# Splitting the late weight blocks of an attention and gated-layer kernel during attention, and keeping them in DRAM

## The chip, the cores and the metric

One core of a Trainium2 chip runs the whole program. The metric is device time in microseconds for one execution. The engines are TensorE (PE; PEld is its loading of stationary operands), VectorE (DVE), ScalarE (ACT), GpSimd (POOL) and SyncE (SP), which issues nearly all DMAs. Every engine takes its instructions in the order in which they were written for it, and SP its DMA issues too.

## The reference

```python
# q, k, v: [4, 8, 768, 64]; proj: [64, 6]; w_gate, w_val: [512, 1536]; w_out: [1536, 512]; w_* in float64
q_bits = (einsum('bhsd,dk->bhsk', q, proj) > 0);  k_bits likewise
mask = q_bucket[:, :, :, None] == k_bucket[:, :, None, :]      # bucket: the 6 bits as a number
scores = where(mask, q @ k.T / sqrt(64), -1e9)
attn = softmax(scores);  attn_out = attn @ v
x = attn_out.transpose(0, 2, 1, 3).reshape(3072, 512)
gate = 1 / (1 + exp(-(x @ w_gate)));  val = x @ w_val
return (gate * val) @ w_out
```

## The kernel before

**Attention.** 16 pairs of heads: b from 0 to 3, and hp from 0 to 3 within each b. A pair is done in two groups g = 0, 1 of three 128-row tiles. A tile has scores (sc), a maximum (DVE, into e and st) and an exponential (ACT). A group has transposes of e (tp, copied to ef by ACT or DVE), sums spread by a product (rs, rb), and the product with v (pv). `summed` (DVE) makes xs from pv, and `store` sends xs to the DRAM tensor xd[b], whose second half of columns is g = 1.

**The gated layer** runs over units of 384 tokens: (b, g), eight in all, each of which needs x of all four pairs of b for its g. `load_x` loads x of a unit (xr), ACT makes its high part xh and DVE or GpSimd the low part xl, each in four chunks of 128 features; there is one buffer for xr and one for xh and xl. Every product is taken as three matmuls: high by low, low by high, high by high. The feed-forward width of 1536 is cut into 12 blocks j. `moe_early` does blocks 0 to 3 of all units: zg (gate) and zv (value), `gated` (gf on DVE, gh on ACT, gl on DVE or GpSimd), then zo (three row tiles, 12 matmuls each), which goes to DRAM as part[b]. `moe_late` does blocks 4 to 11 of all units after attention (names with l, and yo), fetches part and adds it. The early part of unit (2,1) is held back until score tile 82 of the 96 is written (HOLD).

**The weights** come as float64 pairs of 32-bit words. `load_w` loads a raw block of 512 KB (rawg, rawv, rawo) and makes its value by integer and float steps: `exponent`, `mantissa`, `whole`, `signed` on DVE, `shifted` on ACT, `scaled` on GpSimd or DVE, and then its high part (`high`, ACT) and low part (`low`, GpSimd or DVE). The 12 early blocks (j < 4, of g, v and o) are made during attention, in buffers that last through the kernel. The 24 late blocks are loaded and made after `switch`, which closes the pools of attention and gives their space to the late weights.

**The order** on every engine is made when the program is built, by a planner (`Plan`). A task has an engine, an assumed duration, a key, and stocks of buffers that it takes and gives. Of the tasks that are ready on an engine, the one with the lowest key is written next. Keys of attention count score tiles; the early units have 1e4, the late ones 2e4, and products that only fill time 1e5. The planner takes 2000 ns and 1 ns for every 200 bytes as the landing time of a DMA, with 600 ns for the issue and at most eight in flight, and orders by these assumptions:

```python
def dma(key, nbytes, emit, **kw):
    return add(key, "sp", 600, emit, tail=2000 + nbytes // 200, **kw)
```

Of the kernel before, what the change touches and what calls it, by code (L numbers as in the profile page):

```python
# [9 lines left out]
F32 = mybir.dt.float32  # L10
F32R = mybir.dt.float32r
BF16 = mybir.dt.bfloat16
I32 = mybir.dt.int32
# [6 lines left out]
P = 128  # L20
# [32 lines left out]
class Plan:  # L53
# [6 lines left out]
    def add(self, key, engine, ns=None, emit=None, after=(), take=(), give=(), tail=0):  # L60
        options = engine if isinstance(engine, list) else [(engine, ns, emit)]
        t = Task((key, len(self.tasks)), options, after, take, give, tail)
        self.tasks.append(t)
        return t
# [80 lines left out]
def lsh_attention_glu_kernel(ctx, tc, q, k, v, proj, w_gate, w_val, w_out, out):  # L145
    nc = tc.nc
    B, H, S, D = q.shape
# [10 lines left out]
    J1 = 4  # L158
# [10 lines left out]
    xd = [dram.tile([HP, P, S], F32, name=f"xd{b}") for b in range(B)]  # L169
    part = [dram.tile([NG, GT, P, DM], F32, name=f"part{b}") for b in range(B)]  # L170


    ps = ctx.enter_context(tc.tile_pool(name="ps", bufs=4, space=PSUM))
    ident = const.tile([P, P], F32, name="ident")
# [52 lines left out]
    def busy():  # L227
        nc.tensor.matmul(idle, zero[:, :P], zero, start=True, stop=True)

    W_KEY, W_STEP = 31.24, 4.87  # L230
    stock = dict(
        one=3, two=2, moe=1, z=2, kr=2, qr=2, vr=2, h=2, e=10, st=3, su=3, rb=2, xs=2,
        ef=14, raw1=1, mid1=1, raw2=2, mid2=2, xr=1, x=1, ob=3,
    )
    plan = Plan(stock)
    add = plan.add
# [6 lines left out]
    def dma(key, nbytes, emit, **kw):  # L243
        return add(key, "sp", 600, emit, tail=2000 + nbytes // 200, **kw)
# [2 lines left out]
    N_EL = KC * P  # L247
    weights = {}
    made = {}

    def load_w(key, n, j, early, after=()):

        z = {}
        raw_name = "raw1" if early else "raw2"
        pools = lambda: (stage1, w1) if early else (later["stage"], later["w"])

        def load():
            z["raw"] = raw = pools()[0].tile([P, 2 * N_EL], I32, name=f"raw{n}{j}", tag="wraw")
            if n == "o":
                nc.sync.dma_start(raw, w_out[j * P : (j + 1) * P, :])
            else:
                w = w_gate if n == "g" else w_val
                nc.sync.dma_start(
                    raw.rearrange("p (c f) -> p c f", c=KC),
                    w[:, 2 * j * P : 2 * (j + 1) * P].rearrange("(c p) f -> p c f", p=P),
                )  # L270
            pairs = raw.rearrange("p (n two) -> p n two", two=2)
            z["low"], z["high"] = pairs[:, :, 0], pairs[:, :, 1]

        def exponent():
            z["ex"] = pools()[0].tile([P, N_EL], I32, name=f"ex{n}{j}", tag="wex")
            nc.vector.tensor_scalar(z["ex"], z["high"], 0x7FF00000, None, op0=ALU.bitwise_and)

        def shifted():
            nc.scalar.activation(z["ex"], z["ex"], AF.Relu, scale=8.0, bias=ebias)

        def mantissa():
            z["mf"] = pools()[0].tile([P, N_EL], I32, name=f"mf{n}{j}", tag="wmf")
            nc.vector.tensor_scalar(
                z["mf"], z["high"], 0x000FFFFF, 0x00100000, op0=ALU.bitwise_and, op1=ALU.bitwise_or
            )

        def whole():
            nc.vector.scalar_tensor_tensor(
                f(z["mf"]), z["low"].bitcast(U32), 2.0**-32, z["mf"], op0=ALU.mult, op1=ALU.add
            )  # L290

        def signed():
            nc.vector.scalar_tensor_tensor(
                z["ex"], z["high"], SIGN, z["ex"], op0=ALU.bitwise_and, op1=ALU.bitwise_or
            )

        def scaled(eng):
            eng.tensor_mul(f(z["ex"]), f(z["mf"]), f(z["ex"]))

        def high():  # L300
            weights[n, j] = tuple(
                pools()[1].tile([P, N_EL], F32R, name=f"w{n}{x}{j}", tag=f"w{n}{x}{j}") for x in "hl"
            )
            nc.scalar.copy(weights[n, j][0], f(z["ex"]))

        def low(eng):
            hi, lo = weights[n, j]
            eng.tensor_sub(lo, f(z["ex"]), f(hi))

        mid = "mid1" if early else "mid2"  # L310
        a = dma(key, 524288, load, after=after, take=[raw_name])
        b1 = add(key, "dve", 340, exponent, after=[a], take=[mid])
        b2 = add(key, "act", 620, shifted, after=[b1])
        c1 = add(key, "dve", 340, mantissa, after=[b1])
        c2 = add(key, "dve", 610, whole, after=[c1])
        d = add(key, "dve", 610, signed, after=[b2, c2], give=[raw_name])
        pick = lambda fn: [("pool", 1230, lambda: fn(nc.gpsimd))] + (
            [] if early else [("dve", 610, lambda: fn(nc.vector))]
        )
        e = add(key, pick(scaled), after=[d])  # L320
        h = add(key, "act", 520, high, after=[e])
        made[n, j] = add(key, pick(low), after=[h], give=[mid])


    sig = mp.tile([P, J1, GN], F32, name="sig")
# [88 lines left out]
    def moe_early(key, b, g, stored, held=()):  # L414

        u = f"{b}_{g}"
        x = load_x(u, b, g, stored)
        prev, zs = held, []
        for j in range(J1):
            z, prev = product(key, u, "g", j, x, prev, False)  # L420
            zs.append(add(
                FIRST, "act", 375, lambda j=j, z=z: nc.scalar.copy(sig[:, j], z["acc"][:, :GN]),
                after=[prev, sig_free[j]], give=z["bank"],
            ))
        s_ = add(FIRST, "act", 3900, lambda: nc.scalar.activation(sig, sig, AF.Sigmoid), after=zs)
        ready = []
        for j in range(J1):
            z, prev = product(key, u, "v", j, x, prev, j == J1 - 1)
            z["gf_free"] = gf_last[0]
            gf_last[0] = gated(u, j, z, prev, s_)  # L430
            ready.append(gf_last[0])
        for t in range(GT):
            z = {}

            def part_(j, t=t, z=z):
                if j == 0:
                    z["acc"] = ps.tile([P, 512], F32, name=f"zo{t}_{u}", tag="one")
                out_product(z["acc"], j, j, t, j == 0, j == J1 - 1)

            def store(eng, t=t, z=z):  # L440
                z["ob"] = mp.tile([P, DM], F32, name=f"ob{t}_{u}", tag="ob", bufs=stock["ob"])
                eng(z["ob"], z["acc"])

            for j in range(J1):
                prev = add(
                    key if j == 0 else OPEN, "pe", 3 * MO, lambda j=j, fn=part_: fn(j), after=[prev, ready[j], made["o", j]],
                    take=["moe", "one"] if j == 0 else [],
                )
            a = add(FIRST, "act", 480, lambda fn=store: fn(nc.scalar.copy), after=[prev] + in_turn["ob"],
                    take=["ob"], give=["moe", "one"])  # L450
            in_turn["ob"] = [a]
            parts[b, g, t] = dma(
                FIRST, 262144, lambda t=t, z=z: nc.sync.dma_start(part[b][g, t], z["ob"]),
                after=[a], give=["ob"],
            )
        for j in range(J1):
            g_free[j] = prev
# [61 lines left out]
    sp = lambda t: t.rearrange("p (j n) -> p j n", j=2)  # L519
    heads = [(b, hp) for b in range(B) for hp in range(HP)]  # L520
    score_tasks = {}
    stored = {b: [] for b in range(B)}
    halves = [slice(0, D), slice(D, P)]


# [87 lines left out]
    def group(i, g, z, needs, v_here):  # L613
# [138 lines left out]
                give=["ef"] * 2 + (["vr"] if c == NC - 1 and g == NG - 1 else []),  # L752
            )
        a = add(n - 4, "dve", 470, summed, after=[prev, spread_], take=["xs"], give=["one", "rb"])
        stored[b].append(dma(n, 196608, store, after=[a], give=["xs"]))

    WARM, FILL = 8, 60
    for m in range(FILL):
# [1 line left out]
    LAG = 4.2  # L760
    for i in range(len(heads)):
        pair(i)
    every = [s_ for b in range(B) for s_ in stored[b]]

    for m, (n, j) in enumerate((n, j) for n in "gvo" for j in range(J1)):
        load_w(W_KEY + W_STEP * m, n, j, True)
    HOLD = len(heads) * NC - 14
    units = [(b, g) for b in range(B) for g in range(NG)]
    for m, (b, g) in enumerate(units):

        moe_early(1e4 + m, b, g, stored[b], score_tasks[HOLD] if (b, g) == (B - 2, NG - 1) else None)

    def switch():
        ph1.close()
        later["stage"] = ctx.enter_context(tc.tile_pool(name="stage2", bufs=2))
        later["w"] = ctx.enter_context(tc.tile_pool(name="w2", bufs=1))
        later["ps"] = ctx.enter_context(tc.tile_pool(name="ps3", bufs=2, space=PSUM))

    later["switch"] = add(0, "sp", 0, switch, after=every + [made[n, j] for n in "gvo" for j in range(J1)],
                          give=["moe"] * 3)  # L780
    for j in range(J1, NJ):
        for n in "gvo":
            load_w(1e3, n, j, False, after=[later["switch"]])
    ends = {}
    for m, (b, g) in enumerate(units):
        moe_late(2e4 + m, b, g, stored[b], ends)
    ends["end"](ends["prev"])

    for _, emit, _, _ in plan.order():
# [31 lines left out]
```

## Time and profile before

| | |
|---|---|
| median of 3 runs | 1177.62 us (1177.05 to 1177.81) |
| profiled execution | 1176.68 us, its span 1174.9 us |
| mean granted clock of TensorE | 0.993 |
| busy, share of the span | PE 97%, DVE 47%, ACT 47%, POOL 19% |
| bytes moved | HBM read 56.63 MB, written 18.87 MB |

The span goes from the first to the last instruction; the execution's time also has what lies around it. In the trace attention ends at about 683 us. The numbers of the sums in the prediction are us from the start of the span. In rows of stretches the numbers after the limits are the length, then busy us and instructions by engine, then granted clock, share of the 16 DMA engines and GB/s.

### The profile page before, as it was taken

How to read it: one execution, taken by the hardware profiler on the slowest of the kernel's cores; microseconds unless marked ns; L12 is line 12 of the kernel's file. 1: busy time of each engine (PE TensorE's matmuls, PEld its weight loads, DVE VectorE, ACT ScalarE, POOL GpSimd, SP SyncE). 2: the span in 40 equal slices, each digit the busy share in tenths (PEclk: the TensorE clock that was granted, in tenths of full speed). 3: DMA queues.
4: the chain of work that ended last, by engine and by line, in shares of the span. 5: the costliest groups of instructions: out<-in, count | busy, mean ns of one | idle time of the engine just before them, and what ended most of it. 6: DMA issues, size and time to landing. Idle time of an engine off the chain costs nothing.

```text
span 1174.9 us, 17438 instructions
## 1 busy us (share of the span) xinstructions
PE 1143.6 (97%) x6999; PEld 876.5 (75%) x7004; DVE 550.0 (47%) x1202; ACT 550.7 (47%) x1094; POOL 218.0 (19%) x190
## 2 busy tenths in 40 slices
PE   9999999999999999999999958899999999999998
PEld 4655657777657777657677647788999999999997
DVE  5777665545465544455545449996020211202021
ACT  4778776546576555576646525533121221212111
POOL 1223100201000201000201026655121221212121
PEclk9999999999999999999999979999999999999999
DMA  7334222211212211211010044452020202202010
GB/s 171 88 105 113 58 65 59 63 39 34 75 55 61 64 39 35 75 55 35 30 46 7 35 139 144 152 161 92 26 81 1 81 4 77 80 2 81 1 54 27
DMA packets 92657, 76.63 MB, mean 65 GB/s; under 512 B 53152, under 2 KB 81824, under 8 KB 92576
## 3 DMA queue, kind: packets, MB, share of 16 engines
q1 hardware_dynamic: 92416, 75.51, 21.5%
q8 instruction: 55, 0.90, 0.3%
q14 instruction: 26, 0.21, 0.1%
q10 hardware_dynamic: 160, 0.00, 0.0%
HBM read 56.63 MB, written 18.87 MB: 64 GB/s over the span
## 4 chain that ended last, share of the span: by engine, by line
PE 85%; DVE 7%; POOL 3%; issue 2%; ACT 2%; DMA 1%; SPq 1%; POOLq 0%; DVEq 0%; ACTq 0%
PE sc L625 12%; PE tp L692 11%; PE pv L703 11%; PE zv_1l L375 5%; PE zg_1l L375 5%; PE yo_1l L408 5%; PE zg L375 5%; PE zv_0l L375 5%; PE zo L408 4%; PE zv L375 4%; PE zg_0l L375 4%; PE yo_0l L408 4%; PE sc L633 2%; PE rs L679 2%; PE hq L561 2%
## 5 line engine op out<-in xcount | busy, mean ns | idle before, releaser
L663 ACT ACTIVATE e<-e,st 128x768 f32<-128x768 f32 x192 | 196.3, 1024 | 44.6 <-DVE st L655 39.3
L643 DVE TENSOR_SCALAR_CACHE_REDUCE e<-sc 128x768 f32<-128x768 f32 x192 | 176.4, 954 | 85.2 <-PE sc L633 80.9
L696 ACT COPY ef<-tp 128x384 f32<-128x384 f32 x278 | 120.4, 486 | 116.7 <-PE tp L692 115.2
L692 PE MATMUL tp<-ident,e 128*128 128x128 f32 x1152 | 154.3, 276 | 0.5 <-ACT ef L696 0.4
L625 PE MATMUL sc<-kt,qt 64*128 64x384 f32 x768 | 149.8, 508 | 0.0
L692 PEld LDWEIGHTS tp<-ident,e 128*128 128x128 f32 x1152 | 127.9, 141 | 28.1 <-issue 19.8
L703 PE MATMUL pv<-ef,vr 128*64 128x384 f32 x768 | 129.6, 487 | 0.0
L625 PEld LDWEIGHTS sc<-kt,qt 64*128 64x128 f32 x768 | 66.1, 186 | 59.6 <-issue 19.6
L703 PEld LDWEIGHTS pv<-ef,vr 128*64 128x64 f32 x768 | 53.7, 137 | 58.3 <-issue 57.7
L391 DVE TENSOR_TENSOR gf_1l<-zv_1l,sig 128x384 f32<-128x384 f32 x32 | 17.8, 558 | 166.5 <-PE zv_1l L375 166.5
L396 POOL TENSOR_TENSOR gl<-gf,gh 128x384 fp32r<-128x384 f32 x29 | 31.0, 1069 | 326.5 <-ACT gh L395 326.5
L391 DVE TENSOR_TENSOR gf_0l<-zv_0l,sig 128x384 f32<-128x384 f32 x32 | 17.8, 555 | 126.1 <-PE zv_0l L375 126.1
L696 DVE COPY ef<-tp 128x384 f32<-128x384 f32 x106 | 56.6, 554 | 42.7 <-PE tp L692 41.9
L507 ACT ACTIVATE sig<-zg_1l 128x384 f32<-128x384 f32 x32 | 15.7, 492 | 96.2 <-PE zg_1l L375 96.2
L396 POOL TENSOR_TENSOR gl<-gf_1l,gh 128x384 fp32r<-128x384 f32 x32 | 33.4, 1045 | 147.6 <-ACT gh L395 147.6
L348 POOL TENSOR_TENSOR xl<-xr,xh 128x384 fp32r<-128x384 f32 x19 | 20.9, 1120 | 194.0 <-ACT xh L345 194.0
L375 PE MATMUL zg<-xh,wgl 128*128 128x384 f32 x128 | 46.8, 366 | 10.2 <-ACT xh L345 10.2
L396 POOL TENSOR_TENSOR gl<-gf_0l,gh 128x384 fp32r<-128x384 f32 x28 | 30.6, 1094 | 108.4 <-ACT gh L395 108.4
L507 ACT ACTIVATE sig<-zg_0l 128x384 f32<-128x384 f32 x32 | 15.6, 489 | 72.2 <-PE zg_0l L375 72.2
L633 PEld LDWEIGHTS <-qb 12*128 12x128 bf16 x384 | 9.6, 90 | 52.3 <-issue 52.3
L375 PE MATMUL zg<-xl,wgh 128*128 128x384 f32 x128 | 45.0, 351 | 3.4 <-DVE xl L348 2.6
L395 ACT CAST gh<-gf_1l 128x384 fp32r<-128x384 f32 x32 | 16.4, 512 | 64.6 <-DVE gf_1l L391 64.6
(148 smaller groups left out, 2508.7 us busy)
## 6 DMA issues: line engine op xcount, KB each, us to landing
vr<-in_v_dram SPq DMA_DIRECT2D x16, 384.0 KB, 3.5
rawg<-in_moe_w_gate_dram SPq DMA_DIRECT2D x12, 512.0 KB, 3.5
xd<-xs SPq DMA_DIRECT2D x32, 192.0 KB, 3.4
rawv<-in_moe_w_val_dram SPq DMA_DIRECT2D x12, 512.0 KB, 3.5
rawo<-in_moe_w_out_dram SPq DMA_DIRECT2D x12, 512.0 KB, 3.5
xr<-xd SPq DMA_DIRECT2D x8, 768.0 KB, 4.8
part<-ob SPq DMA_DIRECT2D x24, 256.0 KB, 2.0
kr<-in_k_dram SPq DMA_DIRECT2D x30, 192.0 KB, 3.7
```

Of the source, the lines that this page charges most:

```text
L375: nc.tensor.matmul(z["acc"][:, :GN], a[:, wc], x[xx][:, c, :], start=(c == 0 and i == 0), stop=(c == KC - 1 and i == 2),)
L391: nc.vector.tensor_mul(z["gf"], z["acc"][:, :GN], sig[:, j])
L396: low = lambda eng: eng.tensor_sub(gl[:, j], z["gf"], f(gh[:, j]))
L408: nc.tensor.matmul(acc, a[:, slot, ts_], w, start=(first and i == 0), stop=(last and i == 2))
L507: lambda slot=slot, z=z: nc.scalar.activation(sig[:, slot], z["acc"][:, :GN], AF.Sigmoid),
L625: nc.tensor.matmul(sc[h][:, j, :GN], z["qt"][rows, c], z["kt"][rows, j * GN : (j + 1) * GN], start=True, stop=False, tile_position=(h * D, 0),
L633: nc.tensor.matmul(sc[h][:, j, :GN], z["qb"][rows, c], z["kb"][rows, :], start=False, stop=True, tile_position=(at_, 0),)
L643: nc.vector.tensor_scalar(sp(e), gz["sc", t][h][:, :, :GN], -SCALE, None, op0=ALU.mult, op1=ALU.min, accum_out=gz["st", t][:, 0, h : h + 1],)
L663: nc.scalar.activation(e, e, AF.Exp, bias=st[:, 2, h : h + 1], scale=st[:, 1, h : h + 1], accum_out=gz["su"][:, h, t : t + 1],)
L692: nc.tensor.transpose(tp[:, t * P : (t + 1) * P], gz["e", t, h][:, c * P : (c + 1) * P], ident)
L696: copy(gz["ef", c, h], gz["tp", c, h][:, :GN])
L703: nc.tensor.matmul(gz["pv"][rows, :GN], z["v"][:, h, c], gz["ef", c, h], start=(c == 0), stop=(c == NC - 1), tile_position=(0, h * D),)
```

## The change

All 24 late blocks are now loaded and split during attention, on the same buffers as the early ones (one raw, one of intermediate values), after the 12 early blocks. `scaled` and `low` are always on GpSimd. High and low part of a block stand in one tile; a late block's tile (wk, one buffer) is stored in a DRAM tensor `kept` of its own (`keep`, 512 KB in rows of 4 KB). After `switch` each late block is fetched from there (`fetch`, 512 KB) into its place, and nothing more is done to it. The keys of the blocks start at 12.0 and go up by 2.2. A unit (b, g), early or late, waits for the four stores of its own g in place of all eight of b. `switch` waits for all stores of attention and all 24 `keep`s.

```diff
+    kept = {(n, j): dram.tile([P, 2, DM], F32, name=f"k{n}{j}") for n in "gvo" for j in range(J1, NJ)}
...
-    W_KEY, W_STEP = 31.24, 4.87
+    W_KEY, W_STEP = 12.0, 2.2
...
-        ef=14, raw1=1, mid1=1, raw2=2, mid2=2, xr=1, x=1, ob=3,
+        ef=14, raw1=1, mid1=1, wk=1, xr=1, x=1, ob=3,
...
         def high():
-            weights[n, j] = tuple(
-                pools()[1].tile([P, N_EL], F32R, name=f"w{n}{x}{j}", tag=f"w{n}{x}{j}") for x in "hl"
-            )
-            nc.scalar.copy(weights[n, j][0], f(z["ex"]))
+            if early:
+                z["w"] = w1.tile([P, 2, N_EL], F32R, name=f"w{n}{j}", tag=f"w{n}{j}")
+                weights[n, j] = z["w"][:, 0], z["w"][:, 1]
+            else:
+                z["w"] = stage1.tile([P, 2, N_EL], F32R, name=f"w{n}{j}", tag="wk", bufs=stock["wk"])
+            nc.scalar.copy(z["w"][:, 0], f(z["ex"]))
...
+        def keep():
+            nc.sync.dma_start(kept[n, j], f(z["w"]))
+
+        def fetch():
+            w = later["w"].tile([P, 2, N_EL], F32R, name=f"w{n}{j}", tag=f"w{n}{j}")
+            weights[n, j] = w[:, 0], w[:, 1]
+            nc.sync.dma_start(f(w), kept[n, j])
...
+        e = add(key, "pool", 1230, lambda: scaled(nc.gpsimd), after=[d])
+        h = add(key, "act", 520, high, after=[e], take=[] if early else ["wk"])
+        made[n, j] = add(key, "pool", 1230, lambda: low(nc.gpsimd), after=[h], give=["mid1"])
+        if not early:
+            a = dma(key, 524288, keep, after=[made[n, j]], give=["wk"])
+            fetches.append(((n, j), a, fetch))
...
-        stored[b].append(dma(n, 196608, store, after=[a], give=["xs"]))
+        stored[b, g].append(dma(n, 196608, store, after=[a], give=["xs"]))
...
-        moe_early(1e4 + m, b, g, stored[b], score_tasks[HOLD] if (b, g) == (B - 2, NG - 1) else None)
+        moe_early(1e4 + m, b, g, stored[b, g], score_tasks[HOLD] if (b, g) == (B - 2, NG - 1) else None)
...
-    later["switch"] = add(0, "sp", 0, switch, after=every + [made[n, j] for n in "gvo" for j in range(J1)],
+    later["switch"] = add(0, "sp", 0, switch, after=every + [a for _, a, _ in fetches],
                           give=["moe"] * 3)
-    for j in range(J1, NJ):
-        for n in "gvo":
-            load_w(1e3, n, j, False, after=[later["switch"]])
+    for w, a, fetch in fetches:
+        made[w] = dma(1e3, 524288, fetch, after=[a, later["switch"]])
```

SP at the end of attention, before. xd3 with xs3_3_0 and xs3_3_1 are the stores of the last two groups, xr3_0 and xr3_1 the loads of x of units (3,0) and (3,1), and raw the raw weight blocks with their j:

```order
L713 DMA xd3_65<-xs3_3_0_7080 128x384
L713 DMA xd3_65<-xs3_3_1_7173 128x384
L338 DMA xr3_0_7176<-xd3_65 128x4x384
L267 DMA rawg4_7190<-in_moe_w_gate_dram 128x4x256
L267 DMA rawv4_7192<-in_moe_w_val_dram 128x4x256
L264 DMA rawo4_7218<-in_moe_w_out_dram 128x1024
L338 DMA xr3_1_7231<-xd3_65 128x4x384
```

The same place now, where kg4 is the kept tensor of block 4 of the gate and wg4 its place in SBUF:

```order
L722 DMA xd3_65<-xs3_3_0_7426 128x384
L347 DMA xr3_0_7504<-xd3_65 128x4x384
L722 DMA xd3_65<-xs3_3_1_7523 128x384
L318 DMA wg4_7552<-kg4_70 128x1024
L347 DMA xr3_1_7557<-xd3_65 128x4x384
L318 DMA wv4_7562<-kv4_78 128x1024
L318 DMA wo4_7569<-ko4_86 128x1024
```

The load of x of unit (3,0) has moved ahead of the last store, and no raw load stands at this place.

SP further on, around the load of x of the first late unit (xr0_0l), before:

```order
L264 DMA rawo5_7322<-in_moe_w_out_dram 128x1024
L267 DMA rawg6_7378<-in_moe_w_gate_dram 128x4x256
L267 DMA rawv6_7422<-in_moe_w_val_dram 128x4x256
L338 DMA xr0_0l_7430<-xd0_62 128x4x384
L264 DMA rawo6_7469<-in_moe_w_out_dram 128x1024
L453 DMA part3_69<-ob0_3_0_7490 128x512
```

And now:

```order
L318 DMA wg11_7702<-kg11_77 128x1024
L318 DMA wv11_7708<-kv11_85 128x1024
L318 DMA wo11_7717<-ko11_93 128x1024
L347 DMA xr0_0l_7743<-xd0_62 128x4x384
L462 DMA part3_69<-ob0_3_0_7772 128x512
L462 DMA part3_69<-ob1_3_0_7793 128x512
```

Before, eight of the 24 raw loads were ahead of this x; now all 24 fetches are, and the stores of part come behind it.

ACT around the conversion of that x (xh0_0l), before:

```order
L304 CAST wvh7_7656<-exv7_7597 128x512
L395 CAST gh_136<-gf1_3_1_7662 128x384
L345 CAST xh0_0l_7671<-xr0_0l_7430 128x384 x4
L395 CAST gh_136<-gf2_3_1_7680 128x384
L279 ACTIVATE exg8_7705<-exg8_7705,ebias_92 128x512
L395 CAST gh_136<-gf3_3_1_7707 128x384
```

And now:

```order
L404 CAST gh_160<-gf1_3_1_7887 128x384
L354 CAST xh0_0l_7901<-xr0_0l_7743 128x384 x3
L404 CAST gh_160<-gf2_3_1_7909 128x384
L354 CAST xh0_0l_7901<-xr0_0l_7743 128x384
L404 CAST gh_160<-gf3_3_1_7933 128x384
L516 ACTIVATE sig_159<-zg4_0_0l_7913 128x384
L451 COPY ob0_3_1_7957<-zo0_3_1_7897 128x512
```

The steps of the weights are gone from here; the conversion stands ahead of the last two gh of unit (3,1), as it did.

More of the change, by code (lines that the diff above doesn't have):

```diff
@@ L249, in lsh_attention_glu_kernel, with load_w @@
     made = {}
-    def load_w(key, n, j, early, after=()):
+    fetches = []
+    def load_w(key, n, j, early):
         z = {}
-        raw_name = "raw1" if early else "raw2"
-        pools = lambda: (stage1, w1) if early else (later["stage"], later["w"])
         def load():
-            z["raw"] = raw = pools()[0].tile([P, 2 * N_EL], I32, name=f"raw{n}{j}", tag="wraw")
+            z["raw"] = raw = stage1.tile([P, 2 * N_EL], I32, name=f"raw{n}{j}", tag="wraw")
             if n == "o":
@@ L274, in exponent @@
         def exponent():
-            z["ex"] = pools()[0].tile([P, N_EL], I32, name=f"ex{n}{j}", tag="wex")
+            z["ex"] = stage1.tile([P, N_EL], I32, name=f"ex{n}{j}", tag="wex")
             nc.vector.tensor_scalar(z["ex"], z["high"], 0x7FF00000, None, op0=ALU.bitwise_and)
@@ L281, in mantissa @@
         def mantissa():
-            z["mf"] = pools()[0].tile([P, N_EL], I32, name=f"mf{n}{j}", tag="wmf")
+            z["mf"] = stage1.tile([P, N_EL], I32, name=f"mf{n}{j}", tag="wmf")
             nc.vector.tensor_scalar(
@@ L300, in high @@
         def high():
-            weights[n, j] = tuple(
-                pools()[1].tile([P, N_EL], F32R, name=f"w{n}{x}{j}", tag=f"w{n}{x}{j}") for x in "hl"
-            )
-            nc.scalar.copy(weights[n, j][0], f(z["ex"]))
-        def low(eng):
[L307 to L312, printed above, removed]
+            if early:
[4 more added lines that the diff above has]
+            nc.scalar.copy(z["w"][:, 0], f(z["ex"]))
+        def low(eng):
+            eng.tensor_sub(z["w"][:, 1], f(z["ex"]), f(z["w"][:, 0]))
+        def keep():
[4 more added lines that the diff above has]
+            nc.sync.dma_start(f(w), kept[n, j])
+        a = dma(key, 524288, load, take=["raw1"])
+        b1 = add(key, "dve", 340, exponent, after=[a], take=["mid1"])
         b2 = add(key, "act", 620, shifted, after=[b1])
@@ L315, in load_w @@
         c2 = add(key, "dve", 610, whole, after=[c1])
[L316 to L322, printed above, removed]
+        d = add(key, "dve", 610, signed, after=[b2, c2], give=["raw1"])
+        e = add(key, "pool", 1230, lambda: scaled(nc.gpsimd), after=[d])
[4 more added lines that the diff above has]
+            fetches.append(((n, j), a, fetch))
     sig = mp.tile([P, J1, GN], F32, name="sig")
@@ L521, in lsh_attention_glu_kernel @@
     score_tasks = {}
-    stored = {b: [] for b in range(B)}
+    stored = {(b, g): [] for b in range(B) for g in range(NG)}
     halves = [slice(0, D), slice(D, P)]
@@ L762, in lsh_attention_glu_kernel @@
         pair(i)
-    every = [s_ for b in range(B) for s_ in stored[b]]
-    for m, (n, j) in enumerate((n, j) for n in "gvo" for j in range(J1)):
-        load_w(W_KEY + W_STEP * m, n, j, True)
+    every = [a for s_ in stored.values() for a in s_]
+    order = [(n, j) for n in "gvo" for j in range(J1)] + [(n, j) for j in range(J1, NJ) for n in "gvo"]
+    for m, (n, j) in enumerate(order):
+        load_w(W_KEY + W_STEP * m, n, j, j < J1)
     HOLD = len(heads) * NC - 14
@@ L769, in lsh_attention_glu_kernel @@
     for m, (b, g) in enumerate(units):
-        moe_early(1e4 + m, b, g, stored[b], score_tasks[HOLD] if (b, g) == (B - 2, NG - 1) else None)
+        moe_early(1e4 + m, b, g, stored[b, g], score_tasks[HOLD] if (b, g) == (B - 2, NG - 1) else None)
     def switch():
         ph1.close()
-        later["stage"] = ctx.enter_context(tc.tile_pool(name="stage2", bufs=2))
         later["w"] = ctx.enter_context(tc.tile_pool(name="w2", bufs=1))
         later["ps"] = ctx.enter_context(tc.tile_pool(name="ps3", bufs=2, space=PSUM))
-    later["switch"] = add(0, "sp", 0, switch, after=every + [made[n, j] for n in "gvo" for j in range(J1)],
+    later["switch"] = add(0, "sp", 0, switch, after=every + [a for _, a, _ in fetches],
                           give=["moe"] * 3)
-    for j in range(J1, NJ):
-        for n in "gvo":
-            load_w(1e3, n, j, False, after=[later["switch"]])
+    for w, a, fetch in fetches:
+        made[w] = dma(1e3, 524288, fetch, after=[a, later["switch"]])
     ends = {}
     for m, (b, g) in enumerate(units):
-        moe_late(2e4 + m, b, g, stored[b], ends)
+        moe_late(2e4 + m, b, g, stored[b, g], ends)
     ends["end"](ends["prev"])
```

## The prediction

> **What bounds the kernel now.** I read the page first, then the waits of TensorE, then its busy time stage by stage.
>
> ```profile
> span 1174.9 us, 17438 instructions
> PE 1143.6 (97%) x6999; PEld 876.5 (75%) x7004; DVE 550.0 (47%) x1202; ACT 550.7 (47%) x1094; POOL 218.0 (19%) x190
> PE 85%; DVE 7%; POOL 3%; issue 2%; ACT 2%; DMA 1%; SPq 1%; POOLq 0%; DVEq 0%; ACTq 0%
> ```
>
> TensorE is the bound: 97% busy, 85% of the chain that ended last. The number of matmuls does not change, so only the time in which TensorE stands or runs slowly can be won. The stretches below give busy time by engine (PE, PEld, DVE, ACT, POOL), granted clock, DMA share and GB/s. The third to fifth rows run from the end of attention on.
>
> ```profile
> 57.30:140.00 82.70, 82.15 (x607) 48.48 (x608) 60.88 (x158) 66.58 (x141) 20.37 (x16) 1.00 0.32 91
> 160.00:400.00 240.00, 240.00 (x1632) 167.65 (x1631) 125.64 (x315) 146.50 (x292) 20.32 (x21) 1.00 0.21 58
> 682.99:707.18 24.19, 11.87 (x49) 10.64 (x50) 13.88 (x19) 7.47 (x14) 9.10 (x6) 0.72 0.52 171
> 707.20:815.00 107.80, 97.03 (x483) 86.08 (x482) 99.41 (x123) 51.43 (x92) 65.13 (x46) 0.98 0.41 132
> 815.00:1170.00 355.00, 353.73 (x1843) 327.34 (x1843) 60.05 (x90) 66.21 (x136) 72.32 (x68) 1.00 0.14 45
> ```
>
> Attention keeps TensorE full (0.55 us lost in the first row, none in the second). After the late weights are done it is full again (1.27 us lost in 355). The loss lies between 683 and 815, where DVE is 92% busy (99.41 of 107.8) with the late blocks. The waits of TensorE over the whole run (total, times, longest) name who is late there:
>
> ```profile
> PE zg L375 <- ACT xh L345: 10.2, 1, 10.2
> PE zo L408 <- DVE gl L396: 3.9, 3, 1.8
> PE zg L375 <- DVE xl L348: 2.6, 2, 1.4
> PE zv_0l L375 <- DVE gf_0l L391: 1.9, 1, 1.9
> PE zo L408 <- POOL gl L396: 1.5, 2, 1.4
> PE yo_0l L408 <- DVE gl L396: 1.2, 2, 0.8
> ```
>
> The first is the load of x for unit (3,0). It stands in SP's queue behind the store of the last group, and runs beside two raw weight blocks. The others are DVE and GpSimd busy with the split.
>
> **What goes.** The rows of TensorE at the seam, then clock and DMA there:
>
> ```profile
> 678.90 4.04 PE L703 MATMUL pv<-ef,vr 128*64 128x384 f32 x24
> 693.18 0.69 PE L375 MATMUL zg<-xh,wgl 128*128 128x384 f32 x1 [10.24 <-ACT xh L345]
> 707.18 0.33 PE L375 MATMUL zv<-xh,wvl 128*128 128x384 f32 x1
> 715.50 0.39 PE L408 MATMUL zo<-woh,gl 128*128 128x512 f32 x1
> 715.73 0.40 PE L408 MATMUL zo<-wol,gh 128*128 128x512 f32 x1
> ...
> 688.00:690.00 2.00, 0.00 (x0) 0.00 (x0) 0.00 (x0) 0.00 (x0) 0.00 (x0) 0.52 0.96 310
> 702.00:704.00 2.00, 2.00 (x13) 2.00 (x12) 0.57 (x1) 0.79 (x2) 1.72 (x1) 1.00 1.07 386
> 718.00:720.00 2.00, 1.34 (x4) 0.92 (x5) 2.00 (x2) 0.00 (x0) 2.00 (x2) 0.70 0.00 0
> 720.00:722.00 2.00, 2.00 (x8) 1.81 (x7) 2.00 (x4) 0.52 (x1) 0.36 (x2) 0.50 0.05 7
> 686.00:690.00 4.00, 0.00 (x0) 0.00 (x0) 0.00 (x0) 0.00 (x0) 0.00 (x0) 0.76 0.97 325
> ```
>
> Between 707.18 and 715.50 lie 48 products: 8.32 us, 0.173 each. A zo product takes 0.23 (715.50 to 715.73). So:
> - Standing from 682.99 (the last pv's end without its drain) to 693.18: 10.2 us.
> - The 48 zg products of unit (3,0) take 14.0 us (693.18 to 707.18) where 8.3 would do, in holes and at a clock near 0.5: 5.7 us.
> - Idle from 707.2 to 815 (107.80 less 97.03): 10.8 us.
> - The clock at 718 to 722: half of 2.0 busy us, and 0.3 of 1.34: 1.4 us.
>
> Together 28.1 us, as far as their causes go: no raw load beside x, no split on DVE and GpSimd after 683.
>
> **What comes, term by term.**
>
> (a) x for (3,0) now waits for the store of its own half alone. These rows time it (timeline; chain of waits, start and us; DMA issues with median us to landing; groups with busy us and mean ns):
>
> ```profile
> 674.25 0.56 DVE L710 TENSOR_TENSOR xs<-pv,rb 128x384 f32<-128x384 f32 x1 [2.47 <-PE pv L703]
> 674.84 0.32 SPq L713 DMA_DIRECT2D xd<-xs  x1
> 683.65 1.90 DMA xd<-xs
> 686.13 6.54 DMA rawv<-in_moe_w_val_dram
> xd<-xs SPq DMA_DIRECT2D x32, 192.0 KB, 3.4
> rawo<-in_moe_w_out_dram SPq DMA_DIRECT2D x12, 512.0 KB, 3.5
> xr<-xd SPq DMA_DIRECT2D x8, 768.0 KB, 4.8
> L345 ACT CAST xh<-xr 128x384 fp32r<-128x384 f32 x32 | 14.8, 510 | 4.6 <-POOL gl L396 4.6
> L348 POOL TENSOR_TENSOR xl<-xr,xh 128x384 fp32r<-128x384 f32 x19 | 20.9, 1120 | 194.0 <-ACT xh L345 194.0
> ```
>
> The store is issued at 675.2, lands at 677.1 to 678.6 (1.9 to 3.4), x lands 4.8 later, xh takes 0.5 and xl 1.1. The second product can then start at 683.5 to 685.0, TensorE is there at 683.0: 0.5 to 2.5 us with the later chunks, taken 1.3.
>
> (b) The units start a group of heads earlier, so zo of unit (2,1), which fills gaps in the last pair before, is done by then; the last group and a half of attention have nothing beside them. The nearest row is the bare first stretch, with 0.55 us lost in 82.7: -0.5 (the first bare stretch is shorter now) to 2, taken 0.5.
>
> (c) 24 blocks are split during attention. Four blocks of one kind, exponent tile, then mantissa tile (DVE, ACT and POOL; DVE and POOL):
>
> ```profile
> 0.00:145.00 145.00, 4.43 (x8) 5.29 (x8) 10.17 (x8) 1.00 0.40 106
> 0.00:145.00 145.00, 4.46 (x8) 5.09 (x4) 1.00 0.40 106
> ```
>
> So a block costs DVE (4.43+4.46)/4 = 2.2 us, ACT 1.3, POOL 2.5 (the second row's POOL time is in the first already); 24 cost 53, 32 and 61. They are covered: from 160 to 400 DVE is 52% busy, ACT 61%, POOL 8%. If the cover fails, TensorE waits for st, ef and e. In 57.30 to 140, where 8 blocks (16 POOL instructions) were split beside bare attention with DVE at 74% and ACT at 81%, 0.55 us were lost: 24 at that rate are 1.7. SP also gets 24 stores; each waits for POOL with loads of q, k, v, x and the stores of attention behind it, and 12.6 MB more are written beside a DMA share of 0.2 to 0.3. Two buffers of q, k and v cover a late load; a late x would stop TensorE. 0 to 5 (three times the nearest row), taken 1.0.
>
> (d) Units (3,0) and (3,1) still follow each other with the chain gf, gh, gl, and x of the second can be converted only when the first lets go. Nearest rows: 1.27 us in 355 without split work, and 5.4 for zo with it: 0.4 to 3, taken 1.5.
>
> (e) **The unhidden one.** In SP's order the 24 fetches, of 524 KB each, stand ahead of the load of x for the first late unit. Behind the issue at 685.6 (the last store lands: 683.65 + 1.90) go 24 fetches, x of (3,1) and x of (0,0): 14.16 MB. At 325 GB/s, the 4 us row above, that is 43.6 us; with 1.9 fixed (3.5 for 512 KB less 1.6 at that rate) x lands at 731.1, and the second product can start 1.6 later, at 732.7. From 684.3, with (a), TensorE has 192 zg and zv products of the two units and 42 of zo ahead of it: 192 x 0.1735 + 42 x 0.23 = 43.0 us, and with (d) it is there at 728.8. So 2.9 us and some for chunks: 3.5. The ends: at 386 GB/s (the row at 702) x lands in time: 0. At 212 GB/s, the lowest rate of a full queue, below, x lands at 754.3: 27. I take 325, the same queue at the same place with rows of 1 KB and more. While ACT waits for this x, gh of (3,1) and sig stand behind it, and on SP the part stores; TensorE would wait for the x at that point anyway.
>
> (f) The clock fell about 5 us after the stop at 683, but also at 718 after two waits of 1.3 and 0.7. Taken 0.7, ends 0 and 3.
>
> Sum: 1.3 + 0.5 + 1.0 + 1.5 + 3.5 + 0.7 = 8.5, so 28.1 - 8.5 = 19.6 us are won. The profiled execution took 1176.68; 1176.68 - 19.6 = 1157.1. The median of the runs is 0.94 above it: 1158.0.
>
> The Trainium skill, DMA: Bandwidth & Descriptors, section Bandwidth, puts the limit of transfers between HBM and SBUF at about 358 GB/s for a core. By it the 14.16 MB take an estimated 39.6 us, 4 less, term (e) is 0 and the sum 1154.5; the trace's 325 at a share of 0.97 leans to that side of my value, its 386 goes past it.
>
> **Rivals.**
> 1. The fetches are hidden, and TensorE reaches late unit (0,0) after its x: (e) and (f) are 0, (c) and (d) at their low ends: 1152. The row of 386 GB/s speaks for it, that of 325 against.
> 2. The split in attention is not covered: an in-order engine or SP's queue, waiting for POOL, holds back e, ef or an x load. Half a microsecond for each of the 24 blocks: 12 in place of 1.0, 1169. The bare stretch speaks against it.
> 3. The seam stays: x of (3,0) is late all the same, since its store and load queue behind others. Half the old stop, 5, and half the loss at the clock, 3, in place of 1.3: 1165. Against it: no raw block is in SP's queue there any more.
> 4. The other side: the train of fetches is slow. Slower than before begins where (e) reaches 3.5 + 19.6 = 23, that is 14.16 MB in 63.2 us, 224 GB/s. This row is the longest full queue in the trace:
>
> ```profile
> 0.00:20.00 20.00, 17.65 (x85) 8.36 (x86) 10.31 (x41) 5.91 (x10) 1.17 (x7) 1.00 0.95 212
> ```
>
> At 212 GB/s (e) is 27 and (f) 3: 1158.0 + 23.5 + 2.3 = 1184. These were loads of q and k in rows of 256 bytes, those of the fetch have 4 KB, so I give it little. [...]
>
> **Chances and range.** My forecast, 1154 to 1163: 0.54. Rival 1: 0.19. Rival 2: 0.12. Rival 3: 0.08. Rival 4: 0.07. A measurement of this kernel can tell about 0.2%, 2.4 us, from no change. Rivals 1 and 3, the forecast and most of 2 are faster: 0.92; 0.02 within; 0.06 slower. The range of 1151 to 1168 leaves out rival 4 and half of rival 2.
>
> **What would show it.** TensorE's wait for xh at the seam falls from 10.2 to under 2 us, and no stretch there has a clock near 0.5 for more than 4 us. DVE is under 30% busy from 685 to 815. TensorE stays full from 60 to 680; if its idle time there is over 5 us, (c) is wrong. From 686 the DMA share is near 1 for about 43 us; xr_0l lands near 731, and the largest single wait of TensorE is zg_0l on xh_0l or xl_0l at about 729, of some 3 us. If that wait is over 10 us the fetch rate was wrong, if there is none, rival 1 holds. I would be most wrong where the fetch train runs far below 325 GB/s.

## The result and the profile after

| | before | after |
|---|---|---|
| median | 1177.34 us (1176.76 to 1177.81, 4 runs) | 1150.50 us (1150.28 to 1150.98, 4 runs) |
| ratio | | 0.9773, 95% interval 0.9756 to 0.9790 |
| profiled execution | 1176.68 us, span 1174.9 | 1150.42 us, span 1148.6 |
| mean granted clock of TensorE | 0.993 | 1.0 |
| HBM read, written | 56.63, 18.87 MB | 69.21, 31.46 MB |

The change wins 26.8 us. The prediction said 1158.0 (1151 to 1168): 7.5 us too slow, and half a microsecond outside its range. Of the 7.5, 0.9 lie outside the span: the prediction put the median of the runs 0.94 above the profiled execution, as it was before, and it is 0.08 above it. The page after, first the span, the busy times and the chain that ended last:

```profile
span 1148.6 us, 17525 instructions
PE 1138.4 (99%) x6999; PEld 873.8 (76%) x7004; DVE 501.1 (44%) x1182; ACT 548.6 (48%) x1093; POOL 231.5 (20%) x211
PE 93%; POOL 2%; ACT 2%; DMA 1%; DVE 1%; issue 1%; POOLq 0%; SPq 0%; DVEq 0%; ACTq 0%
```

TensorE has the same 6999 matmuls and now fills 99% of the span. All its waits after the start of the program (total, times, longest) fit into four rows:

```profile
PE zg L384 <- DVE xl L357: 1.0, 2, 0.6
PE tp L701 <- ACT ef L705: 0.8, 2, 0.4
PE zg_0l L384 <- DVE xl_0l L357: 0.4, 1, 0.4
PE yo_1l L417 <- POOL gl L405: 0.3, 1, 0.3
```

Neither xh at the seam (10.2 us before) nor xh_0l, for which the prediction had the largest wait, is among them. The stretches, columns as before:

```profile
57.30:140.00 82.70, 82.22 (x606) 48.50 (x608) 61.11 (x160) 67.03 (x142) 20.37 (x16) 1.00 0.33 97
160.00:400.00 240.00, 239.49 (x1608) 166.25 (x1606) 168.43 (x399) 167.02 (x326) 77.77 (x65) 1.00 0.46 150
57.30:680.00 622.70, 621.47 (x4256) 419.65 (x4256) 382.40 (x952) 416.23 (x830) 124.77 (x106) 1.00 0.30 95
683.00:815.00 132.00, 130.23 (x682) 119.23 (x679) 22.59 (x34) 34.83 (x66) 27.15 (x26) 1.00 0.40 151
690.00:720.00 30.00, 29.50 (x157) 27.35 (x156) 4.74 (x7) 11.06 (x19) 5.21 (x5) 1.00 1.03 408
```

Attention carries all 36 blocks (DVE 168.43 us busy in 160 to 400, 125.64 before) and TensorE loses 1.2 us in 622.7. From 683 to 815 DVE is 17% busy; before, it was 92% busy in the stretch from 707.2 to 815. In 690 to 720 the fetches move 408 GB/s. SP's issues of the first fetch and of the load of x for late unit (0,0), and that load's time to landing:

```profile
687.52 0.32 SPq L318 DMA_DIRECT2D wg<-kg  x1
714.78 0.37 SPq L347 DMA_DIRECT2D xr_0l<-xd  x1
xr_0l<-xd SPq DMA_DIRECT2D x1, 768.0 KB, 11.1
```

It lands at 714.78 + 11.1 = 725.9. ACT converts it only at 728.90, when the last zv of unit (3,1) lets go of the one buffer for xh:

```profile
728.90 1.34 ACT L354 CAST xh_0l<-xr_0l 128x384 fp32r<-128x384 f32 x3 [2.86 <-PE zv L384]
```

So this load has 3.0 us to spare. TensorE's rows at the same points as those shown of before, at that late unit, and at the start of the second late unit (0,1):

```profile
680.80 4.04 PE L712 MATMUL pv<-ef,vr 128*64 128x384 f32 x24
684.77 0.44 PE L384 MATMUL zg<-xh,wg 128*128 128x384 f32 x1
686.56 0.44 PE L384 MATMUL zg<-xl,wg 128*128 128x384 f32 x1 [0.60 <-DVE xl L357]
...
694.31 0.33 PE L384 MATMUL zv<-xh,wv 128*128 128x384 f32 x1
...
728.65 0.39 PE L417 MATMUL zo<-wo,gl 128*128 128x512 f32 x1
728.88 0.63 PE L417 MATMUL zo<-wo,gh 128*128 128x512 f32 x2
730.04 0.33 PE L384 MATMUL zg_0l<-xh_0l,wg 128*128 128x384 f32 x1
...
786.04 0.33 PE L384 MATMUL zg_1l<-xh_1l,wg 128*128 128x384 f32 x1
```

The start of the second late unit before:

```profile
812.41 0.33 PE L375 MATMUL zg_1l<-xh_1l,wgl 128*128 128x384 f32 x1
```

The gap from the last pv to the first zg is 3.97 us, the length of the pv itself; it was 14.28. By the starts of TensorE's matmuls (zv of (3,0) at 707.18 before and 694.31 after, zg_1l of (0,1) at 812.41 and 786.04), the gain stands in these places:

| place | before | after | won | by the prediction |
|---|---|---|---|---|
| last pv starts | 678.90 | 680.80 | -1.9 | -1.5 (b, c) |
| last pv to zv of (3,0): the seam | 28.28 | 13.51 | 14.8 | 14.6 (10.2 + 5.7 - a) |
| zv of (3,0) to zg_1l of (0,1) | 105.23 | 91.73 | 13.5 | 6.5 (12.2 - d, e, f) |
| the rest of the span | 362.5 | 362.6 | -0.1 | 0 |
| sum | | | 26.3 | 19.6 |

The first two places came out nearly as predicted. What is missing stands in the third.

### The profile page after: what moved, and what is told of

The parts are those of the page before. It is cut to its first block, busy times and chain, and to the rows that moved or that the text cites. A ratio compares the mean times of both kernels' runs of the same rounds, so it can differ in the third digit from the quotient of the medians.

```text
span 1148.6 us, 17525 instructions
## 1 busy us (share of the span) xinstructions
PE 1138.4 (99%) x6999; PEld 873.8 (76%) x7004; DVE 501.1 (44%) x1182; ACT 548.6 (48%) x1093; POOL 231.5 (20%) x211
## 3 DMA queue, kind: packets, MB, share of 16 engines
HBM read 69.21 MB, written 31.46 MB: 88 GB/s over the span
## 4 chain that ended last, share of the span: by engine, by line
PE 93%; POOL 2%; ACT 2%; DMA 1%; DVE 1%; issue 1%; POOLq 0%; SPq 0%; DVEq 0%; ACTq 0%
PE sc L634 12%; PE tp L701 11%; PE pv L712 11%; PE zv_0l L384 6%; PE zv_1l L384 6%; PE zo L417 6%; PE zg_0l L384 5%; PE zg_1l L384 5%; PE zv L384 5%; PE yo_0l L417 5%; PE zg L384 5%; PE yo_1l L417 5%; PE rs L688 2%; PE sc L642 2%; PE hq L570 2%; PE idle L230 1%
## 5 line engine op out<-in xcount | busy, mean ns | idle before, releaser
L672 ACT ACTIVATE e<-e,st 128x768 f32<-128x768 f32 x192 | 196.3, 1024 | 49.7 <-DVE st L664 48.6
L384 PE MATMUL zg<-xh,wg 128*128 128x384 f32 x256 | 72.2, 344 | 0.0
L384 PE MATMUL zv<-xh,wv 128*128 128x384 f32 x256 | 71.5, 344 | 0.0
L384 PE MATMUL zg_1l<-xh_1l,wg 128*128 128x384 f32 x256 | 70.9, 337 | 0.0
L384 PE MATMUL zg_0l<-xh_0l,wg 128*128 128x384 f32 x256 | 70.8, 337 | 0.0
L384 PE MATMUL zv_0l<-xh_0l,wv 128*128 128x384 f32 x256 | 70.3, 334 | 0.0
L384 PE MATMUL zv_1l<-xh_1l,wv 128*128 128x384 f32 x256 | 70.2, 334 | 0.0
L405 POOL TENSOR_TENSOR gl<-gf_0l,gh 128x384 fp32r<-128x384 f32 x32 | 33.7, 1055 | 145.1 <-ACT gh L404 145.1
L516 ACT ACTIVATE sig<-zg_1l 128x384 f32<-128x384 f32 x32 | 15.7, 492 | 96.3 <-PE zg_1l L384 96.3
```

The costliest lines, as they stand in the source:

```text
L384: nc.tensor.matmul(z["acc"][:, :GN], a[:, wc], x[xx][:, c, :], start=(c == 0 and i == 0), stop=(c == KC - 1 and i == 2),)
L405: low = lambda eng: eng.tensor_sub(gl[:, j], z["gf"], f(gh[:, j]))
L672: nc.scalar.activation(e, e, AF.Exp, bias=st[:, 2, h : h + 1], scale=st[:, 1, h : h + 1], accum_out=gz["su"][:, h, t : t + 1],)
```

## Experiments

**One part alone: waiting for the own half.** The kernel before, with the list of stores kept by half:

```diff
-        stored[b].append(dma(n, 196608, store, after=[a], give=["xs"]))
+        stored[b, g].append(dma(n, 196608, store, after=[a], give=["xs"]))
...
-        moe_late(2e4 + m, b, g, stored[b], ends)
+        moe_late(2e4 + m, b, g, stored[b, g], ends)
```

The early units' line is changed in the same way.

> The kernel before with one part of the change: units wait for the four stores of their own half; the late blocks are still loaded and split after attention. Theory A (two losses, one behind the other, DVE sets the end of the first late unit): x of unit (3,0) comes in time and TensorE's wait for xh at the seam falls from 10.2 us to under 2, but the split of the 24 blocks still ends at about 810 us with DVE over 90% busy, so that unit (0,0) of the late part ends where it did: the time is 1172 to 1177 us, a gain of at most 5. Rival B (the losses add up): the 13 us of the seam are won whole, 1163 to 1166 us.

Measured: 1179.72 us (1177.05 to 1180.61), 1.0018 [1.0009, 1.0028] of the kernel before: 2 us slower, where even Theory A had a small gain. The wait for xh at the seam is gone (first zg at 684.65), but the waits of TensorE have others at their head, and the stretch after 707 is still DVE's:

```profile
PE zg_0l L375 <- POOL wgl L308: 7.5, 2, 4.8
PE yo_0l L408 <- POOL gl L396: 2.3, 1, 2.3
707.00:815.00 108.00, 93.22 (x422) 82.27 (x420) 98.09 (x122) 47.40 (x84) 60.11 (x45) 0.89 0.41 134
```

DVE has as much to do there as before, 98 us in 108 (99.41 in 107.8). TensorE, earlier at the late units, stands for wgl, and the clock in the stretch falls to 0.89 (0.98 before). The 13 us won at the seam are all given back: zv of (3,0) starts at 693.88 in place of 707.18, but zg_1l of (0,1) at 813.14 in place of 812.41. Where the last 2 us went is not shown.

**The other part alone.** The changed kernel, whose units wait for both halves:

```diff
-        moe_early(1e4 + m, b, g, stored[b, g], score_tasks[HOLD] if (b, g) == (B - 2, NG - 1) else None)
+        moe_early(1e4 + m, b, g, stored[b, 0] + stored[b, 1], score_tasks[HOLD] if (b, g) == (B - 2, NG - 1) else None)
...
-        moe_late(2e4 + m, b, g, stored[b, g], ends)
+        moe_late(2e4 + m, b, g, stored[b, 0] + stored[b, 1], ends)
```

> The changed kernel with units waiting for all eight stores again: only the split during attention, the keeping and the fetching are left of the change. Theory A: the seam's stop comes back in part, x of (3,0) is loaded behind the last store and lands at about 691 us; TensorE waits about 7 us for xh, its clock falls for 2 to 4 us, and the bare last group is filled again (-1): 1158 to 1161 us. Rival B (the losses add up): 1150.5 + 13 = 1163 to 1165 us. Rival C (the train of fetches lies beside this x load and holds it up like the raw loads did): 1163 us or more, with the wait for xh over 9 us.

Measured: 1156.88 us (1155.80 to 1157.42), ratio 0.9826 [0.9812, 0.9841]: 20.9 us by itself, a little more than expected. The stop at the seam stays, with its low clock:

```profile
PE zg L384 <- ACT xh L354: 6.5, 1, 6.5
686.00:688.00 2.00, 0.00 (x0) 0.00 (x0) 0.00 (x0) 0.00 (x0) 0.00 (x0) 1.00 0.87 255
688.00:690.00 2.00, 0.00 (x0) 0.00 (x0) 0.00 (x0) 0.54 (x2) 0.00 (x0) 0.63 1.03 375
690.00:692.00 2.00, 1.58 (x4) 1.19 (x5) 1.58 (x2) 1.21 (x3) 1.95 (x2) 0.50 1.01 389
692.00:694.00 2.00, 2.00 (x8) 2.00 (x7) 0.74 (x1) 0.00 (x0) 0.32 (x1) 0.50 1.02 414
694.00:696.00 2.00, 2.00 (x10) 2.00 (x9) 0.00 (x0) 0.48 (x1) 0.00 (x0) 0.67 1.03 420
```

So the parts don't add up: -2.0 and 20.9 us apart, 26.8 together. The own half is worth 6 us only where no split follows the seam.

**The train made longer.** Behind each fetch, SP also issues a copy of the same block into another DRAM tensor:

```diff
             nc.sync.dma_start(f(w), kept[n, j])
+            nc.sync.dma_start(extra[n, j], kept[n, j])
```

> The changed kernel with a copy of 512 KB from DRAM to DRAM behind each of the 24 fetches, 12.6 MB more ahead of the load of x of the first late unit; the copies are read by nothing. Theory A (at 408 GB/s that load is only 3 to 5 us ahead of its use): 26.7 MB take 65 us, TensorE waits 25 to 30 us for xh_0l or xl_0l, 1175 to 1182 us. Rival B (the train has much room): TensorE waits under 5 us, 1150 to 1155 us.

Measured: 1178.24 us (1176.90 to 1178.98), ratio 1.0004 [0.9995, 1.0013]: the whole gain is gone.

```profile
PE zg_0l L386 <- ACT xh_0l L356: 25.6, 1, 25.6
720.00:750.00 30.00, 11.37 (x64) 10.76 (x62) 1.11 (x2) 3.08 (x5) 2.02 (x2) 0.74 1.01 423
```

The wait that the prediction spoke of is the one that appears. In the changed kernel the train is hidden, but only by the 3.0 us between the landing of x at 725.9 and its conversion at 728.9.

**No split at all.** The late blocks are neither loaded nor split; what is kept and fetched in their place is the early block of the same matrix with number j mod 4, so the values of the late products are others:

```diff
-            nc.sync.dma_start(kept[n, j], f(z["w"]))
+            nc.sync.dma_start(kept[n, j], f(tiles[n, j % J1]))
...
+        if not early:
+            a = dma(key, 524288, keep, after=[made[n, j % J1]])
+            fetches.append(((n, j), a, fetch))
+            return
```

> The changed kernel without the loading and splitting of the 24 late blocks: what is kept and fetched for block j is the split early block j modulo 4, so the late part multiplies by other weights. All 24 stores and fetches remain. Theory A (term (c): the split beside attention costs the 1 to 2 us by which attention ends later than before): attention ends at 683 to 683.5 us in place of 685.0, 1148.5 to 1149 us. Rival B (term (b): the bare last group costs them): it ends at 685 as now, 1150.2 to 1150.8 us.

Measured: 1149.63 us (1149.14 to 1149.97), ratio 0.9766 [0.9749, 0.9782], between the two theories. The last pv starts at 680.29, in place of 680.80: 24 blocks loaded and split beside attention cost 0.5 us there and 0.9 in the total. With the own half alone the last pv started at 680.68, with the split alone (units waiting for both halves) at 679.46. So most of the 1.9 us by which attention ends later than before (678.90) belongs to the new order of the units, not to the split.

**The rows of the kept tensors.** The same bytes are laid out so that a store or a fetch moves rows of 1 KB, 512 or 256 bytes in place of 4 KB (here 1 KB):

```diff
-    kept = {(n, j): dram.tile([P, 2, DM], F32, name=f"k{n}{j}") for n in "gvo" for j in range(J1, NJ)}
+    kept = {(n, j): dram.tile([4, P, DM // 2], F32, name=f"k{n}{j}") for n in "gvo" for j in range(J1, NJ)}
...
-            nc.sync.dma_start(f(w), kept[n, j])
+            nc.sync.dma_start(
+                f(w).rearrange("p h (c e) -> p (h c) e", c=2), kept[n, j].rearrange("c p e -> p c e")
+            )
```

> The changed kernel with the kept blocks laid out so that keep and fetch move rows of 1 KB in place of 4 KB; bytes and number of DMAs are the same. Theory A (the 325 GB/s at the seam of the kernel before came from rows of 1 and 1.5 KB, the 408 of the fetches from rows of 4 KB): the train runs at 320 to 350 GB/s and takes 40 to 44 us, x of the first late unit lands at 730 to 734 us, TensorE waits 2 to 5 us for xh_0l, 1153 to 1156 us. Rival B (the rate hangs on how many DMAs are queued, not on the rows): over 400 GB/s, no such wait, 1150 to 1151 us.

> The same with rows of 512 bytes. Theory A: a rate between 212 and 350 GB/s, near 280: 14.16 MB take 50.6 us, x of the first late unit lands near 740 and TensorE waits about 10 us: 1158 to 1166 us. Theory B: as with 1 KB rows, 350 GB/s and a wait near 2 us: 1153 to 1156 us.

> The late blocks are kept in DRAM so that a store or a fetch moves rows of 256 bytes; nothing else differs from the changed kernel. Theory A: the row's size sets the rate of the train (256-byte rows of q and k moved at 212 GB/s at the program's start, 1 KB rows of the train at 350, 4 KB rows at 408). Then 14.16 MB from about 687.5 take 66.8 us, x of the first late unit lands near 756 and TensorE, free at 730, waits some 26 us for it, with 1 to 3 more at a lower clock: 1176 to 1181 us, so that the change would be worth nothing. Theory B: the 212 belonged to the program's start (few queues filled, rows spread over all heads) and the train runs near 350 GB/s as with 1 KB rows: 1153 to 1156 us.

Of the three kernels in this order, the waits and the same 30 us of the train, and with 1 KB rows also ACT's conversion of the late x, which now starts when that x lands:

```profile
PE zg_0l L388 <- ACT xh_0l L358: 2.2, 1, 2.2
732.39 0.93 ACT L358 CAST xh_0l<-xr_0l 128x384 fp32r<-128x384 f32 x2 [5.77 <-DMA xr_0l<-xd]
690.00:720.00 30.00, 29.50 (x157) 27.33 (x156) 4.74 (x7) 11.07 (x19) 5.22 (x5) 1.00 1.09 350
```

```profile
PE zg_0l L388 <- ACT xh_0l L358: 9.7, 1, 9.7
690.00:720.00 30.00, 29.49 (x157) 27.33 (x156) 4.75 (x7) 11.08 (x19) 5.23 (x5) 1.00 1.11 294
```

```profile
PE zg_0l L388 <- ACT xh_0l L358: 24.0, 1, 24.0
690.00:720.00 30.00, 29.51 (x157) 27.35 (x156) 4.75 (x7) 11.09 (x19) 5.23 (x5) 1.00 1.23 223
```

| row | GB/s in 690 to 720 | wait for xh_0l | median us | ratio |
|---|---|---|---|---|
| 4 KB | 408 | none | 1150.50 | 0.9773 [0.9756, 0.9790] |
| 1 KB | 350 | 2.2 | 1154.05 (1153.22 to 1154.60) | 0.9800 [0.9783, 0.9816] |
| 512 B | 294 | 9.7 | 1161.96 (1161.36 to 1162.36) | 0.9865 [0.9850, 0.9880] |
| 256 B | 223 | 24.0 | 1175.49 (1174.09 to 1177.36) | 0.9984 [0.9975, 0.9994] |

The row's size, of stores and fetches together, moves the kernel from the full gain to nearly none. Attention has little part in it: the last pv starts at 681.42, 681.57 and 681.16, 0.4 to 0.8 us later than with 4 KB. At 512 and 1024 bytes the time lies where Theory A put it; at 256 it lies 0.5 us below that, with the train at 223 GB/s where 212 had been taken.

**How long unit (2,1) is held back.** Its early part, whose zo can fill gaps at the end of attention, is released at another score tile, four later (-10 in place of -14) and in a second kernel ten later (-4):

```diff
-    HOLD = len(heads) * NC - 14
+    HOLD = len(heads) * NC - 10
```

> The changed kernel with the early part of unit (2,1) held back until score tile 86 in place of 82, so that its zv and zo stand between the products of the last pair. Theory A (most of the 1.9 us by which attention ends later come from the last group and a half having nothing beside it): attention ends 1 to 1.5 us earlier, 1149 to 1149.6 us. Rival B (a stretch is bare either way, a pair earlier now, and costs the same): 1150.3 to 1151 us.

> The changed kernel with that unit held until score tile 92: its zo (36 products, 8.2 us) stands between the last pv and zg of unit (3,0), and a pair's worth of attention before is bare. Theory A: the conversion of x of (3,0) is covered by that zo, so the 1.2 us of holes in zg go, and the bare stretch costs what it does now: 1149 to 1149.6 us. Rival B: the longer bare stretch costs more than that, 1151 us or over.

Measured: 1150.12 us (1149.94 to 1150.35) and 1150.58 (1150.27 to 1150.65), ratios 0.9769 [0.9754, 0.9783] and 0.9772 [0.9757, 0.9787]. Theory A's earlier end of attention is not there: with -10 the last pv starts at 681.06 (680.80 in the changed kernel). With -4 it starts at 673.14, and the zo products held back fill the time up to the first zg at 685.41 (684.77 in the changed kernel): they change places, and the sum stays. Theory A's gain is not measured, and neither is the loss that Rival B had for -4. The place of that work is worth 0.4 us at most.

## Why the prediction was off

**The bound.** Right: a gain could only come from TensorE's standing and slow running between 683 and 815, and it came from there and nowhere else.

**(a), the seam.** Right: 14.8 us won there, 14.6 predicted. xh was in time; the xl of a later chunk is waited for by 0.6 at 686.56.

**(b) and (c), attention.** 1.9 us in place of 1.5. The parts were the other way round: the split, given 1.0, costs 0.5 by the kernel without it, and the rest is the order, given 0.5. Rival 2 is out: 1.2 us lost in 622.7.

**(e) and (f), the failed step.** The train of fetches was put at 325 GB/s, "the same queue at the same place with rows of 1 KB and more". That row was a mixture in which the raw gate and value blocks moved in rows of 1 KB and x in rows of 1.5 KB; the fetch has 4 KB. The long trains give 408 GB/s with 4 KB and 350 with 1 KB. Why the row of 4 us lies at 325 and not at 350 is not shown; its single microseconds go from 298 to 381. So x landed at 725.9 and not at 731.1, although the first fetch went out at 687.5 and not at 685.6. The place where TensorE needs it was put 1.2 too early (728.8 predicted, zg_0l at 730.04). (e) was 0 in place of 3.5, and (f) 0 in place of 0.7. The kernel with 1 KB rows shows that the step was right but for the size: TensorE waits 2.2 us for its x, the 15 products from there to the first zv_0l take 1.5 more, most of it at a low clock (5.31 in place of 3.85), and its median is 3.6 us higher. By the Trainium skill, Perfetto Trace Analysis, section Roofline, a core whose partner is idle can pull more than the share of 358 GB/s and is bounded near 435; the trace agrees with that note, at 408, and not with the 358 that the prediction quoted from another page as the limit. Rival 1 is what happened to the fetches. That its 1152 lies only 1.5 above the result is luck: it put (c) and (d) at 0 and 0.4, where 0.5 and 2.1 were measured, and it had the same loss as the forecast, which was too small.

**The size of the loss, a second term that was off.** From zv of (3,0) on, the prediction took the idle time of the busy column and the clock, 10.8 + 1.4 = 12.2. Counted by the distance between starts it was 15.7: 35 products of before start later than the pitch, the usual distance between two starts, of 0.173 (zg, zv) or 0.228 (zo, yo) allows. Some of them:

```profile
717.98 0.44 PE L375 MATMUL zg<-xl,wgh 128*128 128x384 f32 x1 [1.27 <-DVE xl L348]
718.25 0.34 PE L375 MATMUL zg<-xh,wgh 128*128 128x384 f32 x1
719.25 0.80 PE L408 MATMUL zo<-woh,gl 128*128 128x512 f32 x1 [0.66 <-DVE gl L396]
719.85 0.63 PE L408 MATMUL zo<-wol,gh 128*128 128x512 f32 x1
720.27 0.63 PE L408 MATMUL zo<-woh,gh 128*128 128x512 f32 x1
```

Only 11 of the 35 show idle time ahead of them in the timeline, 10.5 us in all. A matmul's row is longer than its pitch (0.39 against 0.23 in the zo rows of 728.65 and 728.88), so an idle time is shown too short by about 0.17 each (11 x 0.17 = 1.9). The other 24 start 3.3 us late in all: eight of them at the low clock (719.85 to 722.27, 1.5 us), and most of the rest right behind a stop, about 0.1 each. 10.5 shown, 1.9 and 3.3 make 15.7, so the size of the loss was 3.5 too small. By the Trainium skill, Perfetto Trace Analysis, section Identifying the Most-Contended Engine, the busy share of matmuls is not a good measure of how close a kernel is to its limit, since they are pipelined; in this stretch the trace agrees, with 10.5 us shown idle where 15.7 were lost.

**(d).** 1.5 predicted. By the same count, 2.1 us are lost after: eight products start late, from 705.00 to 733.01. So the third place: 15.7 lost before, 2.1 after, 13.6 by this count for the 13.5 won.

**Rival 3** is out: no stop at the seam, clock 1.00. **Rival 4** was out only by the layout: with 256-byte rows the train runs at the 223 GB/s that the prediction gave as its turning point (224), and the kernel is level with before but for 0.16%.

## What to carry over

Price a train of transfers by rows of the same row size, not by the nearest queue in place or time, and ask what lies behind it in the queue: here the layout of a scratch tensor decided between all of the gain and nearly none. Measure a loss on TensorE by the distance between starts, since the busy column showed 10.5 of 15.7 us here. Where two waits follow each other, a late x and a late weight, removing the first alone can win nothing: here TensorE only moved on to the second, while removing the second alone won 20.9 of the 26.8 us.

## What the runs showed of the hardware

**A row costs a fixed time.** An estimate from the four rates of the train, over 16 DMA engines: a row of 256 bytes took an engine 18.4 ns, 512 bytes 27.9, 1 KB 46.8 and 4 KB 160.6 (256 x 16 / 223, and so on). The steps are 9.5 ns for each 256 bytes all the way, so about 8.9 ns are fixed for each row, and the rate without them would be 432 GB/s. The packets' own times in the traces agree: the median is 18 ns for 256 bytes and 46 for 1 KB in the first 20 us of before, and 65 for the 1.5 KB rows of x and 161 for 4 KB in 690 to 720 of the changed kernel. Those first 20 us, the prediction's 212 GB/s, moved 2.9 of their 4.24 MB in rows of 256 bytes and the rest in longer ones. SP's issues of the fetches also grow, to 1.4 us each with 1 KB rows, but the first of that train took 0.37, which suggests that SP waits for the queue and not the queue for SP. The DMA share of the profile did not show the loss: it reads 1.03 at 408 GB/s and 1.23 at 223.

**In these runs the clock fell some microseconds after the start of a stop, even where the stop was over by then.** In the kernel with both halves TensorE was idle from 683.5 and the clock fell near 688.5. In the one with 1 KB rows it was idle for 2.2 us up to 732.95, and the clock fell after work had begun again:

```profile
732.00:734.00 2.00, 0.90 (x4) 0.65 (x4) 1.07 (x3) 1.35 (x4) 0.56 (x1) 1.00 0.12 46
734.00:736.00 2.00, 1.83 (x7) 1.51 (x7) 1.92 (x2) 0.92 (x2) 1.60 (x2) 0.69 0.00 0
736.00:738.00 2.00, 2.00 (x7) 1.70 (x7) 0.62 (x2) 1.00 (x2) 0.76 (x1) 0.50 0.46 38
738.00:740.00 2.00, 2.00 (x12) 1.96 (x11) 0.00 (x0) 0.00 (x0) 0.25 (x1) 0.96 0.92 339
```

So this stop cost 2.2 us and then 1.5 more. With 512-byte rows the stop began at 731.0, at about the same place, and lasted 9.7 us; the clock fell at the same time, near 734.8 (first row below). Shorter stops did not always do it: before, stops of 1.5, 1.8 and 1.9 us that ended at 748.39, 753.10 and 794.21 left the clock at 1.00 (second and third row). In the kernel with the own half alone a stop of 2.0 us that ended at 738.14 was followed by a low clock (fourth row).

```profile
734.00:736.00 2.00, 0.00 (x0) 0.00 (x0) 0.00 (x0) 0.00 (x0) 0.00 (x0) 0.71 1.11 293
747.00:755.00 8.00, 4.70 (x22) 3.80 (x23) 7.96 (x11) 3.49 (x9) 5.32 (x5) 1.00 0.35 120
793.00:800.00 7.00, 5.79 (x30) 5.40 (x31) 6.28 (x10) 3.10 (x6) 2.49 (x3) 1.00 0.37 92
738.00:740.00 2.00, 1.86 (x5) 1.36 (x6) 2.00 (x4) 0.00 (x0) 0.94 (x1) 0.55 0.00 0
```
